# One fused attention and gated-MLP kernel on Trainium2: the first batch's v and u products as plain fp32 matmuls, two more pairs on the sums of v, small work moved to ScalarE, and a new order of all tasks

## The chip, the cores and the metric

The kernel runs on one core of one Trainium2 chip. The metric is the time of one execution on the device, in microseconds (us); what counts is the median of several runs. The trace is that of one profiled execution.

The engines of the core are PE (TensorE, matrix products), DVE (VectorE), ACT (ScalarE), POOL (GpSimd) and SP (SyncE, which here only issues DMAs). Each works through its own instructions in program order; semaphores hold one back until what it reads is there. PEld is the loading of weights into PE, which runs beside the matmuls.

## What is computed

```
# q, k, v: (8 batches, 8 heads, 576 positions, 64)
q_d, k_d, v_d = means over 4 neighbouring positions
out_d   = softmax(scale * q_d @ k_d.T) @ v_d          # 144 positions, then each repeated 4 times
out_loc = softmax(scale * q @ k.T where |i-j| < 4) @ v
x = (repeat(out_d) + out_loc)  as (8, 576, 512)
h = gelu(x @ w_in);  u, v = halves of h                # w_in 512 x 1024
v = layer_norm(v) * g;  v = w_sg @ v + b_sg            # w_sg 576 x 576
out = x + (u * v) @ w_out                              # w_out 512 x 512
```

All is fp32 at full accuracy; the MLP's weights arrive as 64-bit floats.

## The kernel before, in words

**Attention** runs over 32 pairs of heads, numbered g = 0 to 31, four to a batch. For a pair, SP loads q (`lq`), k (`lk`), the pooled v (`lv`) and the windows of v (`lw`). `qs` and `ks` add q and k over four positions. `S`, `Y`, or both as `YS`, are the local and the pooled scores on PE (L629, L650). Then come the softmax (`mx`, `ma`, `mb`, `my`, `ea`, `eb`, `ec`, `re`, `rc`), its normalization (`np` for the local, `nq` for the pooled probabilities, L725 and L728), the transposes `T`, `U`, `t` on PE (L731, L740) with their copies out of PSUM (`pa`, `pb`, `pc`, `pe`), and `D` (`av`, L792 for the pooled part, L808 for the local part). `oe`, `od`, `xa`, `xb` merge both into x. For the first EARLY_D pairs `D` multiplies with the four rows of v that make a mean, one after the other, straight from what was loaded. For all others `vs` adds the four first (L613 and L614 on POOL, L610 on DVE) and `D` needs a quarter of the pooled matmuls. `lv` is issued as four DMAs of 48 rows in the first case, as two of 112 rows in the second.

**The MLP** runs per batch. Each fp32 operand is split into a high part, rounded to fp32r, and a low part, the rest: x by `xh`, `xl` and `xc`, the weights by `wh` and `wl`. A product is then three fp32r matmuls: high by high, high by low, low by high. `v` (L916) makes five tiles of 128 positions (the last has 64) by 512 columns, over four chunks of 128 of the inner dimension. In batch 0 each chunk is a task of its own, `vk<tile>.<chunk>`, and the last is `v0.<tile>`, so that chunk k can start when pair k is done. `u` (L1114) makes eight blocks of 128 by 288, `s` (L1068; in batch 0 by L1114) is the product with w_sg, and `o` (L1243) that with w_out.

**Weights** come as 64-bit words. For each of twelve blocks (`y0` to `y3` for v, `z0` to `z3` for u, `r0` to `r3` for w_out) `wu` and `wq` scale the words' halves, `wb` shifts bits on DVE (L407 and L409), `wt` adds the halves on POOL (L417), which gives the fp32 weight; `wh` and `wl` (L424) split it.

**The order** is a text, `ORDER`: one list of about 2,450 task names, each with the engine it goes to where there is a choice. `place` walks it, hands out the buffers (8 PSUM banks, 10 wide and 38 narrow SBUF buffers) and so fixes each engine's program. Nothing is moved at run time. Every DMA waits until the sixth before it has landed (`DEPTH`), and `lv` waits for the `D` of two pairs before (of one pair before from g = 6 on).

```
fs = range(FAC if early_d else 1)            # L784: 4 or 1 matmuls per pooled block
ops += [(xh, 0, k), (xh, 1, k)] + ([] if last else [(xl, 0, k)])     # L914: three fp32r products
add(N("lv"), dq2, load_v4, [N("D", ahead // 2)], ...)                # L836
```

Of the kernel before, what the change touches and what calls it, by code (L numbers as in the profile page):

```python
# [90 lines left out]
wy0 wuy0 wqy0/V wby0 wty0 wz3 wqz3 wbz3 lk0 lq0 qs0 S0 mx0 lk1 lq1 S1 ks0/P Y0 lq2 ks1/P ia0 ib0 wuz3 wy1 ea0 mx1 wqy1  # L91
my0 ny0 ec0 es0 qs2 lk2 lk3 lq3 wy2 S2 qs1/P mx2 wtz3 ia1 whz3 ib1 Y1 ea1 wz0 re0 why0 wqy2 ks2/P ia2 wlz3 my1 ny1 ec1
wuy1 ib2 rc0 es1 lq4 wuz0 S3 wqz0 lv0 ks3/P qs3/P Y3 np0/V T0 mx3 lw0 nq0 U0 re1/V rc1 np1 lk4 ia3 ib3 nq1 ea3 Y2 qs4/P
wbz0 ea2 T1 pa1 pa0 wtz0 pb0 my2 pc0 small t0 pe0 wby2 wuy2 wty2 ny2 ec2 es2 my3 ny3/V U1 pb1 pc1/V re2 rc2 t1 whz0
ks4/P ec3 pe1 D0 oe0 es3 wby1 re3 od0 nq2 why2 YS4 wy3 wuy3 lq5 np2 wqy3 qs5 lv2 U2 T2 pa2 wty1 xa0 rc3 why1 nq3 t3 xb0
np3 wlz0 my4 ny4 t2 pb2/V wby3 ma4 pc2 lv1 lw1 xh0 xl0/P ec4 U3 wly2 T3 pa3 wty3 mb4 pb3/V wz2 pc3/V lk5 pe2 mx4 pe3 ks5
wqz2 wbz2 wuz2 D1 YS5 ma5 my5 oe1 od1 xa1 xb1 mb5 lw2 mx5 wly0 D2 oe2/V lv4 od2 xh1/V lw3 vk1.0 vk2.0 nx4 eb4 ea4 re4
rc4 lv3 D3 xa2 xl1 wtz2 whz2 wly1 vk1.1 nx5 vs4 ea5 eb5 xb2 xh2 ny5 nq4 wz1 oe3/V od3 xa3 xb3 xh3 xc0 why3 wly3 ec5
vk0.0 vk3.0 vk3.1 xl3/P lk6 vk0.1 lq6 wlz2 np4/V T4 xl2 U4 qs6 wr2 ks6 wqz1 pa4/V re5 rc5 wuz1 vk1.2 wbz1 wtz1 v0.1 wqr2
vg0.1 vk0.2 vk2.1 vk2.2 np5 lw4 pb4 t4 pc4 xc1 pe4 v0.2 wbr2 xc2 vg0.2 wq3 whq3 wq1 D4 vb0.1 vb0.2 xc3 whq1 wlq1 vp0.2  # L100
YS6 ma6 my6 wur2 v0.0 vg0.0 vk4.0 vk4.1 ny6 vk4.2 v0.4 nq5 vk3.2 wq0 whq0/V wlq0 ec6 v0.3 lk8 t5 whz1/V wlz1 mb6 mx6
wlq3 vb0.0 lk7 T5 pa5/V U5 ks7 pb5/V pc5/V va0.4 lq7 vp0.0 oe4/V qs7 vn0.2 lv5 lq8 vs5 od4 xa4 nx6 eb6 ea6 vg0.3 vj0.4
xb4 pe5 ks8 u0.3 vn0.0 u0.4 u0.2 ua0.4 vg0.4 vp0.1 ua0.2 vn0.1/A ua0.3 re6/V lw5 rc6 nq6 u0.5 qs8 wr1 wqr1/V D5 wq2
oe5/V lv6 ua0.5 vh0.0 od5 YS7 my7 ma7 mb7 whq2 t6 xa5 u0.0 vb0.4 np6 U6 vb0.3/A T6 u0.6 vh0.1 xb5 ny7 ec7 wlq2 mx7 wq4
pa6/V pb6 pc6 vs6 whq4 pe6 vl0.1 vh0.2/V vp0.4 lw6 vl0.0 u0.7 vn0.4 u0.1 ua0.6 ua0.7 b vp0.3 vn0.3/A ua0.0 vl0.2 ua0.1
vh0.4/V D6 YS8 wlq4/V nx7 eb7 vh0.3/V vl0.3/P ea7 lv7 lk10 wbr1 wtr2 vl0.4 s0.1 ma8 oe6/V od6 s0.0 xh5 lw7 vs7 s0.5 mb8
my8 ny8 mx8 nx8/V lk9 sa0.1 ec8 re7/V rc7 nq7/V xa6 xb6 np7 wr0 wqr0 wur1 sa0.0 sm0.0/P s0.2 ks10 lq10 lw8 t7 T7 pa7 ks9
U7 s0.3 pb7/V pc7 sm0.1/P pe7/V lq9 sa0.2 eb8 gh0.0/A qs9 sa0.3 sm0.3 ea8 sa0.5 D7 YS9 qs10 wr3 wur3 s0.4 ma9 xl5 re8
rc8 wtr1 s0.6 whr2 mb9 xh4 my9 lv8 oe7 sm0.2/P vs8 lk11 np8 T8 ny9 ec9 sa0.4 nq8/V lw9 xc5 mx9 U8 pa8 pb8 pc8/V t8 pe8
xh6 nx9 wqr3 s0.7 od7 xa7 xb7 eb9 lq11 sm0.5/P D8 lv9 YS10 lk12 sm0.4/P sa0.6 xh7 wur0 xl4/P xc4 xl6/P xc6 sa0.7 sm0.7  # L110
wbr0 xl7 oe8 ea9 my10 ny10/V ks12 wtr0 re9 rc9 ec10 ks11 v1.3 ma10 whr0 gh0.1/A vg1.3 np9/V mb10 mx10 wlr2 sm0.6/P
gh0.3/A br v1.0 nq9 od8 whr1 gl0.1 qs11/P xc7 wbr3 gh0.2/A bd vs9/V v1.1 vg1.1 vb1.1/A gl0.2/V T9 xa8 pa9 t9 wlr1 U9
pb9/V pc9/V pe9 v1.2 xb8 vg1.0 vb1.0/A vg1.2 wlr0/V nx10 vb1.2/A gl0.3/V wtr3 u1.4 lq12 D9 lv10 YS11 gl0.0/V oe9/V vp1.0
gr vn1.0/A vb1.3/A u1.5 ua1.4 whr3 od9 xa9 tq2 my11 qs12/P ma11 mb11 ua1.5 v1.4 ny11 ec11 vs10 tq3 xb9 mx11 vp1.1
vn1.1/A tq4 bs wlr3/V be nx11 eb10 eb11 tq1 o0.2 o0.1 ea10 ea11 u1.6 ua1.6 vp1.3 vn1.3/A vp1.2 o0.6 gt o0.4 o0.0 re10
# [1381 lines left out]
```

## Time and profile before

| | |
|---|---|
| median of 3 runs | 561.27 us (560.44 to 561.32) |
| profiled execution | 562.39 us, span of the trace 560.6 us |
| PE busy | 536.9 us, 96% of the span |
| DVE, ACT, POOL busy | 483.5 (86%), 417.4 (74%), 364.0 (65%) |
| DMA | 64.50 MB, mean 115 GB/s |

The span is the time from the first to the last instruction of the trace; the execution's own time has 1.8 us around it. The profile also cuts the span into 40 slices of 14 us and gives each engine's busy tenths: PE shows 6, 8, 5 and 8 in the first four and 9 in nearly all others. The clock that PE was granted is near full speed in all slices but the third and fourth, where it reads 8 tenths.

### The profile page before, as it was taken

How to read it: one execution, taken by the hardware profiler on the slowest of the kernel's cores; microseconds unless marked ns; L12 is line 12 of the kernel's file. 1: busy time of each engine (PE TensorE's matmuls, PEld its weight loads, DVE VectorE, ACT ScalarE, POOL GpSimd, SP SyncE). 2: the span in 40 equal slices, each digit the busy share in tenths (PEclk: the TensorE clock that was granted, in tenths of full speed). 3: DMA queues.
4: the chain of work that ended last, by engine and by line, in shares of the span. 5: the costliest groups of instructions: out<-in, count | busy, mean ns of one | idle time of the engine just before them, and what ended most of it. 6: DMA issues, size and time to landing. Idle time of an engine off the chain costs nothing.

```text
span 560.6 us, 17562 instructions
## 1 busy us (share of the span) xinstructions
PE 536.9 (96%) x6864; PEld 499.9 (89%) x6864; DVE 483.5 (86%) x1008; ACT 417.4 (74%) x1384; POOL 364.0 (65%) x441
## 2 busy tenths in 40 slices
...
GB/s 314 237 234 318 170 82 278 53 67 105 158 176 122 2 154 110 47 136 42 157 108 77 100 90 122 155 45 57 118 144 135 36 101 109 50 1 2 64 21 107
DMA packets 31923, 64.50 MB, mean 115 GB/s; under 512 B 3808, under 2 KB 4832, under 8 KB 31840
## 3 DMA queue, kind: packets, MB, share of 16 engines
q1 hardware_dynamic: 31840, 63.37, 36.0%
...
q14 instruction: 29, 0.24, 0.1%
...
## 4 chain that ended last, share of the span: by engine, by line
PE 82%; DVE 8%; DMA 6%; issue 3%; ACT 1%; SPq 1%; DVEq 0%; ACTq 0%
PE ps L1114 19%; PE ps L916 17%; PE ps L1068 16%; PE ps L1243 14%; PE ps L792 4%; PE ps L808 3%; PE ps L629 3%; PE ps L731 3%; DMA R<-in_qT_dram 3%; PE ps L650 2%; PE ps L740 2%; DMA R<-in_kT_dram 1%; DMA weight_z<-in_w_in_dram 1%; DMA weight_y<-in_w_in_dram 1%; SPq L240 1%
## 5 line engine op out<-in xcount | busy, mean ns | idle before, releaser
L1114 PE MATMUL ps<-X,weight_z 128*128 128x288 f32 x512 | 109.2, 298 | 1.6 <-DVE X L637 1.6
L916 PE MATMUL ps<-weight_y,X 128*128 128x512 f32 x320 | 97.3, 398 | 0.1
L689 ACT ACTIVATE X<-X,nb 128x64 f32<-128x64 f32 x280 | 93.6, 339 | 1.2 <-DVE nb L668 0.8
L1114 PEld LDWEIGHTS ps<-X,weight_z 128*128 128x128 f32 x512 | 84.1, 188 | 2.2 <-DVE X L637 1.8
L1114 PE MATMUL ps<-R,weight_z 128*128 128x288 f32 x256 | 75.5, 295 | 0.0
L916 PEld LDWEIGHTS ps<-weight_y,X 128*128 128x128 f32 x320 | 58.5, 188 | 12.7 <-ACT R L1142 0.4
L1068 PE MATMUL ps<-wsg_h,R 128*128 128x288 f32 x266 | 58.4, 300 | 0.3 <-ACT pd L711 0.3
L248 ACT CAST R<-R 128x576 fp32r<-128x576 f32 (+2 forms) x77 | 48.0, 646 | 13.7 <-DVE R L1105 5.9
L1250 DVE TENSOR_TENSOR R<-ps,R 128x288 f32<-128x288 f32 x98 | 41.9, 448 | 16.8 <-PE ps L1243 16.6
L689 ACT ACTIVATION_READ_ACCUMULATOR X<-X,nb 128x1 f32 x280 | 53.4, 191 | 0.0
L248 ACT COPY R<-ps 128x464 f32<-128x464 f32 (+4 forms) x94 | 35.0, 412 | 23.2 <-PE ps L731 10.3
L1226 POOL TENSOR_TENSOR R<-R,R 128x576 fp32r<-128x576 f32 x24 | 35.2, 1477 | 26.2 <-ACT R L248 11.7
L916 PE MATMUL ps<-weight_y,R 128*128 128x512 f32 x128 | 50.6, 395 | 0.5 <-DVE R L827 0.5
L1243 PE MATMUL ps<-R,weight_r 128*128 128x288 f32 x336 | 50.3, 297 | 0.0
L1114 PEld LDWEIGHTS ps<-R,weight_z 128*128 128x128 f32 x256 | 48.2, 188 | 0.1
L1243 PEld LDWEIGHTS ps<-R,weight_r 128*128 128x128 f32 x336 | 46.7, 188 | 0.9
L1068 PEld LDWEIGHTS ps<-wsg_h,R 128*128 128x128 f32 x266 | 43.5, 188 | 0.9 <-ACT pd L711 0.6
L1243 PE MATMUL ps<-R,R 128*128 128x288 f32 x252 | 38.6, 299 | 0.8 <-DVE R L470 0.8
L1003 POOL TENSOR_TENSOR R<-R,R 128x512 fp32r<-128x512 f32 (+1 forms) x18 | 24.9, 1393 | 20.9 <-DVE R L248 7.6
L1142 ACT ACTIVATE R<-ps 128x288 f32<-128x288 f32 x64 | 24.5, 412 | 16.8 <-PE ps L1114 15.5
L1243 PEld LDWEIGHTS ps<-R,R 128*128 128x128 f32 x252 | 34.8, 188 | 1.7 <-DVE R L470 1.2
L711 ACT ACTIVATE pd<-ps,nbd 128x144 f32<-128x144 f32 x96 | 35.3, 377 | 0.9 <-DVE nbd L680 0.2
...
## 6 DMA issues: line engine op xcount, KB each, us to landing
...
```

The source lines that it names most:

```text
L248: (nc.scalar.copy if e == "A" else ENG[e].tensor_copy)(**kw)
L689: nc.scalar.activation(out=st["ms"][:, t, :], in_=src, func=AF.Exp, bias=st["nb"][:, t:t + 1], scale=scale, accum_out=sums[par][:, t:t + 1])
L711: nc.scalar.activation(out=pd[:, n], in_=st["sdv"][n].rearrange("p (c k) -> p c k", c=3), func=AF.Exp, bias=st["nbd"][:, n:n + 1], scale=s ...
L792: nc.tensor.matmul(out=out, lhsT=lhsT, rhs=pdt[ks, probs, h * QC:(h + 1) * QC], start=first, stop=last)
L916: nc.tensor.matmul(out=acc, lhsT=r32(l), rhs=r32(weights[f"y{k}"][:, 0, w]), start=(i == 0 and ks[0] == 0), stop=(i == len(ops) - 1 and ks ...
L1003: ENG[e].tensor_tensor(out=r32(dst), in0=vact[s][0][0:n], in1=vh[0:n, 0:DM], op=ALU.subtract)
L1068: nc.tensor.matmul(out=s_bank(j, c), lhsT=r32(l), rhs=r32(r), start=first_in and i == 0, stop=i == len(ops) - 1, skip_group_check=not firs ...
L1114: nc.tensor.matmul(out=acc[:, 0:HALF], lhsT=r32(l), rhs=r32(r), start=(first and n == 0), stop=(last and n == len(ops) - 1))
L1142: nc.scalar.activation(out=gate(i), in_=at["ps", "m", b, "u", i][:, 0:HALF], func=AF.Gelu_apprx_tanh)
L1226: ENG[e].tensor_tensor(out=r32(gl[m]), in0=us[raws[m]], in1=gh[m], op=ALU.subtract)
L1243: nc.tensor.matmul(out=bank(j, c), lhsT=r32(l), rhs=r32(r), start=first and i == 0, stop=i == len(ops) - 1, skip_group_check=not first)
L1250: nc.vector.tensor_tensor(out=x, in0=bank(j, c), in1=x, op=ALU.add)
```

## The change

Five things are changed.

- `EARLY_D` goes from 4 to 2: pairs 2 and 3 add v first (`vs2`, `vs3`), their `lv` are two DMAs of 112 rows, and their `D` have 16 pooled matmul records in place of 64.
- In batch 0 the v and u products are plain fp32 matmuls of x and of the unsplit weight that `wt` leaves: one matmul per chunk in place of three (two in the last v tile). `xh`, `xl` and `xc` are gone for batch 0; chunk k waits for `xb` of pair k and for `wt` of weight k. The splits of the weights stay, for batch 1.
- The last v tile of batch 0 needs no joining of its halves (`va`, `vj` are gone there).
- ACT may do `nq` (as three scaled copies) and `xc`.
- `ORDER` is another list. It starts with loads of q and k where it started with two weights.

```
-EARLY_S, EARLY_D, WIDE, SMALL_O, SMALL_S = 4, 4, 4, 1, 1
+EARLY_S, EARLY_D, WIDE, SMALL_O, SMALL_S = 4, 2, 4, 1, 1
...
+    def unsplit(t):
+        return at["R", "w", t][:, 0:DM]
...
         def norm_d(e):
+            if e == "A":
+                for i in range(3):
+                    nc.scalar.activation(out=st["pdv"][:, i], in_=st["pdv"][:, i], func=AF.Copy,
+                                         scale=st["rc"][:, NT + i:NT + i + 1])
+                return
...
+        if b == 0:
+            return
         add(N("xh"), {"A": 0.64, "V": 0.4}, x_high, ...
...
-        xn = [f"xl{b * NPAIR + p}" for p in range(NPAIR)]
+        xn = [f"{'xb' if first else 'xl'}{b * NPAIR + p}" for p in range(NPAIR)]
...
+                if first:
+                    for k in ks:
+                        l = sb[k]["x"][:, s * P:min(S, (s + 1) * P)]
+                        nc.tensor.matmul(out=acc[0:LEFT] if last else acc, lhsT=l, rhs=unsplit(f"y{k}"), start=k == 0, stop=k == KT - 1)
+                    return
...
+                if first:
+                    acc = buf("ps", "m", b, "u", i)[:, 0:HALF]
+                    for k in range(KT):
+                        l = block(unsplit(f"z{k // 2 * 2 + d}"))[:, k % 2, ds]
+                        nc.tensor.matmul(out=acc, lhsT=l, rhs=sb[k]["x"][:, cs], start=k == 0, stop=k == KT - 1)
+                    return
...
-            w = [f"wly{i}" for i in range(KT)] if first else []
+            w = [f"{'wty' if first else 'wly'}{i}" for i in range(KT)] if b < 2 else []
```

Of the list, the places around pairs 2 and 3 as the engines get them follow. A row names the line, the operation, and what it writes and reads; "x2" is two in a row.

SP before, from pair 2's v (48 rows at a time) to pair 3's v:

```order
L240 DMA R_656<-in_v_dram 48x512 x2
L240 DMA R_657<-in_v_dram 48x512 x2
L240 DMA R_702<-in_v_dram 48x512 x2
L240 DMA R_703<-in_v_dram 48x512 x2
L240 DMA X_708<-in_vw_dram 128x640
L240 DMA weight_z_733<-in_w_in_dram 128x2x512
L240 DMA R_737<-in_kT_dram 128x586
L240 DMA X_845<-in_vw_dram 128x640
L240 DMA R_904<-in_v_dram 112x512
L240 DMA R_905<-in_v_dram 112x512
L240 DMA X_911<-in_vw_dram 128x640
L240 DMA R_934<-in_v_dram 48x512 x2
```

The same stretch of SP in the change:

```order
L240 DMA R_652<-in_v_dram 48x512 x2
L240 DMA X_671<-in_vw_dram 128x640
L240 DMA R_741<-in_qT_dram 128x586
L240 DMA R_750<-in_kT_dram 128x586
L240 DMA weight_y_757<-in_w_in_dram 128x1024
L240 DMA R_760<-in_v_dram 112x512
L240 DMA R_761<-in_v_dram 112x512
L240 DMA R_765<-in_v_dram 112x512
L240 DMA R_766<-in_v_dram 112x512
L240 DMA X_771<-in_vw_dram 128x640
L240 DMA X_833<-in_vw_dram 128x640
```

Pair 5's k (`R_737` before, `R_750` in the change) stood ahead of pair 3's v by six DMAs and still stands ahead of it; pairs 2 and 3 now take four DMAs for v in place of eight, and pair 4's v (`R_904`, `R_905`) has moved behind them.

PE before, where the scores of pair 5 (L629) end and `D2` begins:

```order
L629 MATMUL ps_814<-R_737,R_651 64x64 x2
L629 MATMUL ps_813<-R_737,R_651 64x64 x2
L629 MATMUL ps_814<-R_737,R_651 64x64 x2
L792 MATMUL ps_849<-R_700,R_656 64x144 x2
L792 MATMUL ps_850<-R_700,R_656 64x144 x2
L792 MATMUL ps_849<-R_700,R_656 64x144 x2
```

The same place in the change, where L632 are the scores, L924 the chunks of the plain v product, L748 a transpose and L800 the pooled part of `D2`:

```order
L632 MATMUL ps_791<-R_750,R_741 64x64 x2
L924 MATMUL ps_769<-R_586,R_777 128x512
L748 MATMUL ps_846<-turn_p,pd_102 112x112 x2
L924 MATMUL ps_753<-R_586,R_777 128x512
L924 MATMUL ps_775<-R_586,R_777 128x512
L800 MATMUL ps_863<-R_727,vd_99 64x144 x2
L800 MATMUL ps_864<-R_727,vd_99 64x144 x2
L800 MATMUL ps_863<-R_727,vd_99 64x48 x2
L800 MATMUL ps_864<-R_727,vd_99 64x96 x2
L816 MATMUL ps_863<-R_663,X_771 64x58 x2
```

Three chunks of v now stand between pair 5's scores and `D2` (three more stand ahead of the scores), and `D2` reads the sums `vd_99`.

POOL before, from the normalization of pair 3 (L725) to the sums of v of pair 4 (L613, L614):

```order
L725 TENSOR_TENSOR X_472<-X_472,rc_109 128x640
L424 TENSOR_TENSOR weight_z_542<-R_491,weight_z_542 128x2x256
L827 TENSOR_TENSOR R_712<-R_675,X_710 128x576
L424 TENSOR_TENSOR weight_y_614<-R_516,weight_y_614 128x512
L417 TENSOR_TENSOR R_695<-R_695,weight_y_648 128x512
L424 TENSOR_TENSOR weight_y_361<-R_169,weight_y_361 128x512
L417 TENSOR_TENSOR R_745<-R_745,weight_z_733 128x512
L424 TENSOR_TENSOR weight_y_678<-R_608,weight_y_678 128x512
L613 TENSOR_TENSOR pairs<-R_904 112x256
```

POOL in the change, from the same normalization (L728 there) to the sums of pairs 2 and 3 (L616, L617):

```order
L728 TENSOR_TENSOR X_449<-X_449,rc_109 128x640
L424 TENSOR_TENSOR weight_y_604<-R_582,weight_y_604 128x512
L736 TENSOR_TENSOR pd_102<-pd_102,rc_109 128x9x48
L417 TENSOR_TENSOR R_586<-R_586,weight_y_469 128x512
L424 TENSOR_TENSOR weight_y_638<-R_404,weight_y_638 128x512
L417 TENSOR_TENSOR R_735<-R_735,weight_z_579 128x512
L616 TENSOR_TENSOR pairs<-R_760 112x256
L617 TENSOR_TENSOR vd_99<-pairs 112x128
L616 TENSOR_TENSOR pairs<-R_761 112x256
L617 TENSOR_TENSOR vd_99<-pairs 112x128
L616 TENSOR_TENSOR pairs<-R_765 112x256
L617 TENSOR_TENSOR vd_100<-pairs 112x128
```

The split of x (L827) and two splits of weights have gone from ahead of this place, and the sums of two more pairs have come.

## Rows read from the trace of the kernel before

**Rows 1.** Busy time in stretches: us of each engine (instructions), PE's clock, DMA share, GB/s

```profile
0.00:24.70 24.70, 18.54 (x334) 14.05 (x338) 21.78 (x65) 15.71 (x40) 18.10 (x32) 1.00 0.82 280
24.70:37.47 12.77, 8.73 (x272) 7.51 (x264) 10.93 (x26) 11.32 (x44) 12.69 (x13) 1.00 0.86 253
37.47:45.17 7.70, 5.20 (x127) 5.07 (x128) 3.91 (x9) 3.07 (x17) 5.61 (x7) 0.56 0.80 222
45.17:50.67 5.50, 4.41 (x127) 3.67 (x126) 3.35 (x8) 4.06 (x22) 1.62 (x2) 1.00 1.03 385
52.50:61.39 8.89, 8.89 (x45) 6.95 (x43) 8.30 (x16) 6.73 (x17) 6.19 (x5) 1.00 0.92 265
61.39:112.00 50.61, 50.61 (x841) 48.20 (x841) 45.73 (x104) 47.45 (x170) 42.67 (x53) 1.00 0.46 133
...
140.00:280.00 140.00, 136.87 (x1709) 128.37 (x1709) 130.43 (x267) 115.86 (x381) 95.42 (x114) 1.00 0.35 110
```

**Rows 2.** Timeline of PE, 36 to 53 us: start, duration, what, idle before

```profile
36.76 0.71 PE L650 MATMUL ps<-kd,qd 64*64 64x144 f32 x12 [1.21 <-DVE kd L593]
39.97 0.34 PE L650 MATMUL ps<-kd,qd 64*64 64x48 f32 x1 [2.50 <-issue]
...
46.26 0.56 PE L808 MATMUL ps<-R,X 64*64 64x58 f32 x21 [1.09 <-issue]
...
48.34 1.71 PE L792 MATMUL ps<-R,R 48*64 48x144 f32 x60
...
52.20 0.33 PE L808 MATMUL ps<-R,X 64*64 64x58 f32 x4 [1.52 <-issue]
```

**Rows 3.** Timeline of PE, products of batch 0, a transpose, and D of pair 4

```profile
53.96 0.62 PE L916 MATMUL ps<-weight_y,X 128*128 128x512 f32 x2
...
55.37 0.62 PE L916 MATMUL ps<-weight_y,X 128*128 128x512 f32 x2
...
61.39 0.63 PE L792 MATMUL ps<-R,vd 48*64 48x144 f32 x15
...
68.88 0.43 PE L1114 MATMUL ps<-X,weight_z 128*128 128x288 f32 x2
...
74.45 0.43 PE L1114 MATMUL ps<-X,weight_z 128*128 128x288 f32 x2
...
79.48 0.58 PE L731 MATMUL ps<-turn_l,X 122*128 122x122 f32 x4
```

**Rows 4.** Groups of PE's instructions, 56 to 112 us: busy us, mean ns of one

```profile
L731 PE MATMUL ps<-turn_l,X 122*128 122x122 f32 x25 | 3.6, 267 | 0.0
```

**Rows 5.** Timeline of SP's queue (DMA issues), and the first wait of DVE

```profile
21.70 7.28 SPq L240 DMA_DIRECT2D R<-in_v_dram  x8
...
30.95 1.20 SPq L240 DMA_DIRECT2D R<-in_v_dram  x2
...
34.85 4.10 SPq L240 DMA_DIRECT2D R<-in_v_dram  x4
...
4.83 0.43 DVE L403 TENSOR_SCALAR weight_y<-weight_y 128x512 f32<-128x512 f32 x1 [1.33 <-DMA weight_y<-in_w_in_dram]
```

**Rows 6.** Groups of POOL's instructions, 0 to 52.5 us: busy us, mean ns of one

```profile
L596 POOL TENSOR_TENSOR half<-R 128x288 f32<-128x288 f32 x8 | 5.3, 666 | 0.2
L417 POOL TENSOR_TENSOR R<-R,weight_y 128x512 int32<-128x512 int32 x4 | 5.2, 1297 | 4.6 <-DVE R L409 4.6
L728 POOL TENSOR_TENSOR pd<-pd,rc 128x432 f32<-128x432 f32 x5 | 4.5, 908 | 5.1 <-DVE rc L722 5.1
...
L725 POOL TENSOR_TENSOR X<-X,rc 128x640 f32<-128x640 f32 x3 | 3.8, 1260 | 0.4 <-DVE rc L722 0.4
...
L597 POOL TENSOR_TENSOR kd<-half 128x144 f32<-128x144 f32 x5 | 2.1, 426 | 0.4
...
L613 POOL TENSOR_TENSOR pairs<-R 112x256 f32<-112x256 f32 x2 | 1.5, 738 | 0.0
...
L614 POOL TENSOR_TENSOR vd<-pairs 112x128 f32<-112x128 f32 x2 | 0.9, 456 | 0.2
```

More of the change, by code (lines that the diff above doesn't have):

```diff
@@ L90 @@
 ORDER = """
[L91 to L115, printed above, removed]
@@ new lines @@
+lv0 wz3 ny3 U1 rc2 t1 ec3 re3 pa1 pb1 pc1 pe1 D0 wz0 wby2 wby1 oe0 nq2 np2 T2 wqz0 rc3 od0 xa0 xb0 wty2 why2 YS4 why0 U2
+ma4 t2 np3 lv1 wly2 T3 pa2 mb4 wuy1 my4 pb2 ny4 lw1 D1 pc2/V pe2 wuz0 mx4 pa3 wbz0 ec4 lq5 nq3 U3 pb3 lk5 oe1/V vk2.0
+pc3/V wy3 od1 lv2 wty1 lv3 vk1.0 lw2 wqz3 ks5 vk0.0 xa1 qs5 YS5 wuz3 xb1 wbz3 wly0 wtz0 nx4 vk1.1 my5 vs2 ma5 mb5 lw3
+wqy3 vs3 ea4 t3 pe3/V eb4 re4 vk2.1 ny5 ec5 vk0.1 D2 mx5 wby3 lq6 wtz3 D3 nx5 oe2/V od2 oe3/V vk3.0 lk6 vk3.1 xa2 xb2
+od3 vk3.2 vk0.2 wz1 lk7 wuy3 ea5 whz3/V eb5 vk1.2 whz0 why1/V wty3 why3 wlz3 wqz1 xa3 xb3 v0.1 rc4 vk2.2 re5/V nq4/A rc5
@@ new lines @@
+whq4/V D5 YS7 wlq4 wur2 vb0.4 vp0.4 vl0.2/P wq1 my7 oe5/V U6 ny7/V lw6 pa6 whz1 wlz1 lv6 pb6/V pc6 u0.7 ec7 small u0.0
+ma7 mb7 od5 wq3 whq3 wlq3 xa5 xb5 mx7 vs6/V t6 u0.1 ua0.7 whq1 b pe6/V whz2 lk8 ks8 D6 YS8 vn0.4/A ua0.0 ua0.1 vl0.3/P
+nx7 eb7 lv7 wlq1/V lq10 vh0.4/V xh5/V vl0.4/P xl5/P oe6/V lk10 s0.3 od6 gr wtr1 ma8 mb8 mx8 ea7 re7 nx8/V lq9 eb8 wlz2
+ea8 vs7/V s0.0 rc7 np7 nq7 s0.1 lk9 xa6 xb6 ks10 sa0.0 s0.2 U7 my8 ny8 sa0.1 t7 ec8 qs9 sm0.0/P sa0.2 T7 sm0.1/P sa0.3
+wtr2 pa7 pb7/V pc7/V ks9 sm0.3/P pe7 s0.5 lw7 re8 D7 YS9 wr3 whr1 lk11 lw9 rc8 xh6 np8 sa0.5 lv8 vs8/V ma9 nq8/A mb9 lw8
@@ L874, in attention @@
         add(N("np"), {"P": 1.42, "V": 0.78}, norm, [N("rc")])
-        add(N("nq"), {"P": 0.98, "V": 0.5}, norm_d, [N("rc")])
+        add(N("nq"), {"P": 0.98, "V": 0.5, "A": 1.1}, norm_d, [N("rc")])
         add(N("T"), {"T": 0.44}, turn, [N("np")], takes=[("ps", "t", g, 1)], gives=[("X", "ms", g)])
@@ L927, in emit @@
                 vact[s] = [v]
-                if s == NS - 1:
+                if s == NS - 1 and first:
+                    total = dict(accum_out=sum5[s][0:LEFT]) if by_scalar(s) else {}
+                    nc.scalar.activation(out=v[0:LEFT], in_=acc[0:LEFT], func=AF.Gelu_apprx_tanh, **total)
+                elif s == NS - 1:
                     copy(e, out=v[0:LEFT], in_=acc[LEFT:P])
@@ L1321, in mlp @@
                     add(f"vk{s}.{k}", {"T": c / KT}, v_mm(s, range(k, k + 1)),
-                        xn[k:k + 1] + w[k:k + 1] + (xc[k:k + 1] if last else []) + ([f"vk{s}.{k - 1}"] if k else []),
-                        takes=[] if k else [("ps", "m", b, "v", s)])
+                        xn[k:k + 1] + w[k:k + 1] + ([f"vk{s}.{k - 1}"] if k else []),
+                        takes=[] if k else [("ps", "m", b, "v", s)], gives=[("R", "w", f"y{k}")])
                 add(N("v", s), {"T": c / KT}, v_mm(s, range(k + 1, KT)),
-                    xn[-1:] + w[-1:] + (xc[-1:] if last else []) + [f"vk{s}.{k}"], gives=xs)
+                    xn[-1:] + w[-1:] + [f"vk{s}.{k}"], gives=[("R", "w", f"y{KT - 1}")])
             else:
@@ L1328, in mlp @@
                     gives=xs)
-            if last:
+            if last and not first:
                 add(N("va", s), {"A": 0.58, "V": 0.6}, v_act(s), [N("v", s)], takes=[("R", "v", b, s)])
```

207 lines of the change are left out of this document (112 added, 95 removed).

## The prediction

> **What bounds the kernel now.** Read the stretches first [rows 1]. From 52.5 to 112 us PE is busy without a gap, and from 140 to 280 us for 136.87 of 140 us: PE sets the time there, and only less PE work or fewer of its few waits would help. Before 52.5 it is different. PE is busy for 18.54 of the first 24.7 us and for 8.73 of the next 12.77, while DVE (21.78 and 10.93) and POOL (18.10 and 12.69) are nearly full: there PE waits for the softmaxes and the weights that these two prepare.
>
> Then read PE's timeline around pairs 2 and 3 [rows 2]. It waits 1.21 us for pair 5's pooled k, whose scores stand ahead of `D2` in its program, and then three times, 2.50, 1.09 and 1.52 us, for nothing that the profile shows ("issue"). Between the first two of these there are 127 matmul records [rows 1], between the second and third again 127: PE stops at equal distances in its own program, so I take them for waits for the next block of its code, while the DMA engines are 80% busy and more. From one restart to the next it is 46.26 - 39.97 = 6.3 and 52.20 - 46.26 = 5.9 us: in this traffic a block did not come faster. In the same stretch the granted clock is 0.56 on average [rows 1], so PE ran most of it at 1.2 of its 2.4 GHz, after having been idle for 2.5 us. `D4` starts at 61.39 [rows 3]; from then on I count PE's work only.
>
> **The price of a plain product.** A split v chunk is three fp32r matmuls of 512 columns. Six of them take 55.37 - 53.96 = 1.41 us [rows 3], so one is 0.235, a chunk 0.705 and the last tile (eight matmuls) 1.88. A split u block is twelve of 288 columns: from 68.88 to 74.45 there are 42, 0.1326 each, so 1.59 a block.
>
> No plain fp32 product of full width is in the trace. The nearest are the transposes, plain fp32 and full height: four take 0.58 us [rows 3], of which the last one's own latency is 0.267 [rows 4], so the spacing is 0.313 / 3 = 0.104 us for 122 columns, 0.855 ns a column or two cycles at 2.4 GHz. A plain product leaves two records: `D3` has 60 and then 4 pooled records [rows 2] for 32 products. So a chunk costs 2 x 512 x 0.855 = 0.875 us and a u block 4 x 2 x 288 x 0.855 = 1.97. The bounds: two records at the fp32r pace (0.47 and 1.06) below, four at that pace (0.94 and 2.12) above. I take the transposes because they are the same type at the same height.
>
> The Trainium skill ("FP8 and Floating Point Precision", section TensorE Precision Notes) says that true fp32 takes four passes through the array where the reduced form takes one; that speaks against this change, four against the three of the split. By it a chunk would cost 0.94 and a u block 2.12, and the sum below would end 2.1 us later. The trace agrees in part: two records per product, each at two cycles a column.
>
> So PE's work grows. v: 20 x 0.875 - (16 x 0.705 + 1.88) = +4.3. u: 8 x (1.97 - 1.59) = +3.0. `D2` and `D3` lose 48 records each at 1.71 / 60 = 0.0285 us [rows 2], -2.7. Net +4.6 us. A gain must come from the waits of the first 61 us.
>
> **When D3 can start in the changed order.** Three queues decide.
>
> - POOL. The first q can be there at 5.0 us: the first load, 512 KB, was there at 4.83 [rows 5], and k and q of pair 0 are 586 KB. From then to the sums of pair 3's v the order gives POOL 9 sums of q or k (0.666 + 0.426), 4 x 1.260, 4 x 0.908, 4 weights' `wt` at 1.297, 2 splits of weights, put at the same, and 4 x (0.738 + 0.456) for `vs2` and `vs3` [rows 6]: 9.8 + 5.0 + 3.6 + 7.8 + 4.8 = 31.0. Without a wait that ends at 36.0. I add 1.5 for waits on the first softmax: 37.5.
> - Loads. Up to pair 3's window the change loads twelve q and k (293 KB), six weights (512), 2 x 384 and 2 x 448 of v and four windows (320): 9,532 KB or 9.76 MB, at the 280 GB/s of the first 24.7 us [rows 1] 34.9 us, so landed at 35.6. Pieces of 48 rows hold SP's queue: eight took 7.28 and four 4.10 us, two of 112 rows 1.20 [rows 5]; pairs 2 and 3 save 3.6 + 4.1 - 2 x 1.2 = 5.3 us of that queue. Pair 5's k, the load that PE waited for, comes 1.7 MB sooner (with it, 7,184 KB are loaded in place of 8,892).
> - PE's code. The same count of records puts the next two block ends inside pair 5's scores and inside `D3`. If the first is passed at 33, the second is not before 39 (6.0 on), so `D3`, begun at 37.5, pauses for some 1.4 us.
>
> DVE is close behind POOL; ahead of `D3` it loses one weight's shift, two sums of q, a normalization and a rounding of x and gains a sum of k, so I cost it at no more than POOL's wait. If that cover is gone, `D3` follows DVE instead.
>
> `D3` takes 1.1 as the small `D` do and ends at 37.5 + 1.1 + 1.4 = 40.0. Between it and `D4` PE has ten chunks (8.75) and 14 transposes (1.5): `D4` starts at 50.2, **11.2 us earlier** than 61.39. They have their weights by then: the last one's `wt` is POOL's second task behind `vs3`.
>
> **After D4.** Before, three chunks, the last tile, eight u blocks and a transpose group are left, 2.1 + 1.9 + 12.7 + 0.4 = 17.1; now four chunks and eight u blocks, 3.5 + 15.8 = 19.3: **+2.2**. From 52.5 to 112 us DVE (8.30 + 45.73 of 59.50) and ACT (6.73 + 47.45) are both 91% busy [rows 1], so a PE that runs 9 us ahead will sometimes wait for them: **+2.0**, between -3 (the new order takes work from DVE, where 3.1 us of PE's time is idle from 140 to 280) and +4. `nq` and `xc` on ACT and the last tile without its join I cost at nothing: PE's queue covers them; a single one on the path would be about 1 us, POOL's 0.908 [rows 6] being the nearest.
>
> **Sum.** 560.6 - 11.2 + 2.2 + 2.0 = 553.6 us of span. The median of the runs, 561.27, stood 0.7 above the span (the profiled execution, 562.39, stood 1.8 above), so 554.3 us.
>
> **Rivals.**
>
> 1. *The loads, not the engines, set the pace.* `lv3` may not be issued before `D1` has ended, and both windows stand behind it on SP. If `D1`, which still takes v in 48-row pieces, ends after 38 us, `D3` stays where it was, and PE's added work is all that is left: 561.27 + 4.6 = 565.9, slower. It decides if pair 3's window lands after 47 us, a rate of 211 GB/s; against it, the slowest of the stretches up to 37.47 shows 253 GB/s [rows 1].
> 2. *Part is given back.* PE does little between 12 and 27 us in the new order. If its clock falls as it did from 37.47 on [rows 1], then `D1`, six chunks, pair 5's scores and `D2` (2.2 + 5.25 + 0.9 + 1.1 = 9.5 us at full clock) take up to as much again, of which POOL's queue covers about half. Or ACT and DVE hold PE after `D4` by their upper bound. Either gives some 4.5 more: 558.8, between 556.5 and 562.
> 3. *More is won.* The waits after `D4` end at -3 in place of +2: 549.3.
> 4. *The price is wrong.* At the lower bound ten chunks save 4.1 and the rest 8.9: 541. At the upper one 556.4. Two records at one cycle would contradict the transposes' spacing, so I give the lower end little.
>
> **Chances and range.** Forecast 0.44, rival 2 0.24, rival 3 (with the low price) 0.18, rival 1 (with anything as bad) 0.14. A measurement of this kernel can tell 0.2%, 1.1 us, from no change: 560.2 to 562.4 counts as the same, which takes 0.04 of rival 2. Faster is 0.44 + 0.18 + 0.20 = 0.82, slower 0.14. The range of 547.5 to 562.0 leaves out most of rival 1 and the low price.
>
> **What would show it.** Right: `D3` ended near 40 and `D4` begun near 50; PE without gaps from there; a chunk of L924 every 0.875 us and a block of L1143 every 1.97; one "issue" wait in or near `D3`, not three. Wrong: `D3` after 45 with SP waiting for `D1`; a granted clock near 0.5 between 25 and 40; DVE or ACT as PE's releasers from 50 to 110; chunks at 0.47 or 0.94.

## The result, and the profile after

The changed kernel takes 555.84 us (median of 7 runs, 553.72 to 559.32) where the kernel before, beside it, takes 560.65 (559.36 to 562.61): a ratio of 0.990, with a 95% interval of 0.988 to 0.993. It is 1% faster; 554.3 was forecast, between 547.5 and 562.0. The profiled execution took 556.03 us and its span is 554.2, against 560.6.

The same stretches as in [rows 1], of the kernel after:

```profile
0.00:24.70 24.70, 20.84 (x406) 16.13 (x407) 19.41 (x62) 15.44 (x52) 19.20 (x36) 1.00 0.86 283
24.70:37.47 12.77, 12.07 (x247) 8.53 (x246) 11.62 (x28) 11.37 (x47) 12.15 (x14) 1.00 0.99 274
37.47:45.17 7.70, 7.70 (x125) 4.30 (x125) 7.38 (x18) 7.60 (x33) 6.05 (x7) 1.00 1.04 317
45.17:50.67 5.50, 5.50 (x28) 3.04 (x27) 5.02 (x9) 4.51 (x12) 5.27 (x7) 1.00 1.05 302
...
61.39:112.00 50.61, 49.70 (x688) 42.98 (x687) 48.56 (x100) 46.92 (x156) 41.83 (x43) 1.00 0.57 172
...
140.00:280.00 140.00, 137.68 (x1759) 129.13 (x1760) 122.30 (x244) 118.50 (x403) 95.81 (x117) 0.99 0.34 104
```

From 24.7 to 50.7 us PE is busy for 25.27 of 25.97 us, where it was for some 18, and the granted clock stays at 1.00 through the stretch that had 0.56. But the engines beside PE are now as full as PE: from 37.47 to 45.17 DVE has 7.38 and ACT 7.60 of 7.70 us, and from 61 to 112 DVE has 48.56 of 50.61 where it had 45.73. That will matter.

PE's timeline of the kernel after, the places of [rows 2] and [rows 3] (start, duration, what, idle before):

```profile
27.61 0.47 PE L739 MATMUL ps<-turn_l,X 122*128 122x122 f32 x3 [0.31 <-issue]
...
33.98 0.64 PE L653 MATMUL ps<-kd,qd 64*64 64x144 f32 x13 [0.39 <-DVE qd L596]
...
38.25 0.63 PE L800 MATMUL ps<-R,vd 48*64 48x144 f32 x15
...
40.39 7.13 PE L924 MATMUL ps<-R,R 128*128 128x512 f32 x16
...
50.61 0.63 PE L800 MATMUL ps<-R,vd 48*64 48x144 f32 x15
...
56.04 6.09 PE L1143 MATMUL ps<-R,R 128*128 128x288 f32 x24
...
98.16 0.63 PE L800 MATMUL ps<-R,vd 48*64 48x144 f32 x15
```

`D2` begins at 38.25, `D3` ends with the row before 40.39, `D4` begins at 50.61 (61.39 before), `D8` at 98.16 (106.4 before). Of the three "issue" waits of [rows 2], 5.1 us together, none is left; one of 0.31 has come at 27.3. The eight chunks that begin at 40.39 are followed by a transpose at 47.36, so a chunk is 0.871 us; the three u blocks from 56.04 to 61.96 are 1.973 each.

POOL, then SP's queue, of the kernel after:

```profile
33.17 0.73 POOL L616 TENSOR_TENSOR pairs<-R 112x256 f32<-112x256 f32 x1 [0.39 <-DMA R<-in_v_dram]
...
37.66 0.46 POOL L617 TENSOR_TENSOR vd<-pairs 112x128 f32<-112x128 f32 x1
```

```profile
18.58 1.86 SPq L240 DMA_DIRECT2D R<-in_v_dram  x4
...
26.45 2.50 SPq L240 DMA_DIRECT2D R<-in_v_dram  x4
...
29.39 3.15 SPq L240 DMA_DIRECT2D X<-in_vw_dram  x2
```

The sums of pair 3's v are done at 38.1, and the four DMAs of pairs 2 and 3 hold SP's queue for 2.50 us where eight held it for some 7.7, half of 7.28 and 4.10 [rows 5].

So the lead in the traces is 10.8 us at `D4`, 8.3 at `D8` and 6.4 at the end (between the medians it is 4.8; the profiled execution of the kernel before was one of its slower ones). The rest of this text is on two questions: which part of the change made the 10.8, and what took 4.4 of them away.

### The profile page after: what moved, and what is told of

Same layout as the page of the kernel before. It is cut to its first block, busy times and chain, and to the rows that moved or that the text cites. A ratio compares the mean times of both kernels' runs of the same rounds, so it can differ in the third digit from the quotient of the medians.

```text
span 554.2 us, 17274 instructions
## 1 busy us (share of the span) xinstructions
PE 541.9 (98%) x6720; PEld 492.2 (89%) x6720; DVE 473.6 (85%) x988; ACT 425.7 (77%) x1434; POOL 367.3 (66%) x443
## 4 chain that ended last, share of the span: by engine, by line
PE 82%; DVE 10%; ACT 3%; POOL 3%; issue 1%; ACTq 0%; DVEq 0%; POOLq 0%
PE ps L1086 17%; PE ps L1132 15%; PE ps L1267 14%; PE ps L931 13%; PE ps L800 3%; PE ps L816 3%; PE ps L1143 3%; PE ps L632 3%; PE ps L924 3%; PE ps L739 3%; PE ps L653 2%; PE ps L748 2%; ACT X L692 1%; PE ps L1459 1%; ACT R L248 1%
## 5 line engine op out<-in xcount | busy, mean ns | idle before, releaser
L1132 PE MATMUL ps<-X,weight_z 128*128 128x288 f32 x448 | 96.3, 299 | 0.4 <-ACT R L1166 0.2
L931 PE MATMUL ps<-weight_y,X 128*128 128x512 f32 x280 | 85.0, 397 | 0.5 <-DVE R L409 0.2
L1132 PEld LDWEIGHTS ps<-X,weight_z 128*128 128x128 f32 x448 | 74.3, 190 | 1.4 <-ACT R L1166 0.4
L1132 PE MATMUL ps<-R,weight_z 128*128 128x288 f32 x224 | 66.5, 297 | 0.0
L931 PEld LDWEIGHTS ps<-weight_y,X 128*128 128x128 f32 x280 | 51.0, 188 | 11.3 <-DVE R L1226 0.5
L1021 POOL TENSOR_TENSOR R<-R,R 128x512 fp32r<-128x512 f32 (+1 forms) x26 | 34.2, 1318 | 26.1 <-ACT R L248 7.7
L248 ACT COPY R<-ps 112x192 f32<-112x192 f32 (+4 forms) x86 | 32.4, 411 | 24.4 <-DVE R L248 6.3
L931 PE MATMUL ps<-weight_y,R 128*128 128x512 f32 x112 | 44.1, 394 | 0.0
L613 DVE TENSOR_REDUCE vd<-R 112x128 f32<-112x512 f32 x42 | 43.7, 1082 | 0.3 <-DMA R<-in_v_dram 0.3
L1132 PEld LDWEIGHTS ps<-R,weight_z 128*128 128x128 f32 x224 | 42.6, 190 | 0.0
```

Of the source, the lines that this page charges most:

```text
L248: (nc.scalar.copy if e == "A" else ENG[e].tensor_copy)(**kw)
L613: nc.vector.tensor_reduce(out=vd[:, i], in_=v.rearrange("p f d -> p d f"), axis=AX.X, op=ALU.add)
L931: nc.tensor.matmul(out=acc, lhsT=r32(l), rhs=r32(weights[f"y{k}"][:, 0, w]), start=(i == 0 and ks[0] == 0), stop=(i == len(ops) - 1 and ks ...
L1021: ENG[e].tensor_tensor(out=r32(dst), in0=vact[s][0][0:n], in1=vh[0:n, 0:DM], op=ALU.subtract)
L1132: nc.tensor.matmul(out=acc[:, 0:HALF], lhsT=r32(l), rhs=r32(r), start=(first and n == 0), stop=(last and n == len(ops) - 1))
```

## The experiments

All kernels that were run; D4 and D8 are the starts of these two in the trace, in us. A name that begins with b is an edit of the kernel before, one that begins with a an edit of the changed kernel. Each ran beside the kernel before on the same chip, whose medians were 560.65 to 561.83.

| kernel | median us | ratio to before, 95% interval | span | D4 | D8 |
|---|---|---|---|---|---|
| before | 560.65 | 1 | 560.6 | 61.4 | 106.4 |
| changed | 555.84 | 0.990 (0.988 to 0.993) | 554.2 | 50.6 | 98.2 |
| b_early2 | 560.83 | 0.999 (0.997 to 1.001) | 558.4 | 59.4 | 104.4 |
| b_plain | 568.58 | 1.013 (1.010 to 1.017) | 566.1 | 61.0 | 111.2 |
| b_both | 565.37 | 1.007 (1.004 to 1.009) | 563.6 | 59.7 | 110.0 |
| a_early4 | 564.27 | 1.005 (1.002 to 1.008) | 559.5 | 56.7 | 104.2 |
| b_shift | 563.19 | 1.003 (1.001 to 1.005) | 560.9 | 61.5 | 106.9 |
| a_warm14 | 555.85 | 0.990 (0.986 to 0.994) | 553.6 | 50.6 | 98.1 |
| a_less_u | 557.28 | 0.991 (0.988 to 0.994) | 553.8 | 50.3 | 97.9 |
| a_less_v | 555.89 | 0.989 (0.985 to 0.994) | 553.2 | 49.8 | 97.6 |
| a_less_d | 555.34 | 0.990 (0.988 to 0.992) | 554.8 | 51.0 | 98.5 |
| a_less_ud | 557.97 | 0.993 (0.990 to 0.995) | 557.9 | 52.8 | 100.6 |
| a_np9 | 555.07 | 0.990 (0.988 to 0.991) | 553.1 | 50.8 | 98.4 |
| a_nq_pool | 556.94 | 0.992 (0.990 to 0.994) | 555.4 | 50.6 | 98.7 |

### One part alone, in the old order

**b_early2**, the sums of v for pairs 2 and 3 (on DVE, where the change has them on POOL):

```
-EARLY_S, EARLY_D, ... = 4, 4, ...
+EARLY_S, EARLY_D, ... = 4, 2, ...
-... ks5 wqz2 ... lv3 D3 ...
+... ks5 vs2/V wqz2 ... lv3 vs3/V D3 ...
```

> The kernel before with only EARLY_D = 2 (vs2 and vs3 on DVE, one behind ks5, one behind lv3; order otherwise as before). My theory: this part alone takes 2.7 us of records from PE in D2 and D3 and 96 records out of the stretch with the three issue waits, so that one of them (1.1 to 2.5 us) falls out of it; DVE is idle there and takes the 4 sums. D4 begins 3 to 4 us earlier than 61.39, the time is 557 (556 to 559). Rival A, the end is set by the order of the loads alone: within 1 us of the kernel before. Rival B, small DMA pieces were most of the loss: D4 begins 8 us or more earlier, time below 554.

No change that can be measured. PE's timeline of b_early2, at `D3` and `D4`:

```profile
46.26 0.76 PE L794 MATMUL ps<-R,vd 48*64 48x144 f32 x8 [3.15 <-DVE vd L612]
...
59.35 0.63 PE L794 MATMUL ps<-R,vd 48*64 48x144 f32 x15
```

There is no "issue" wait in this stretch any more, and 96 records fewer. But `D3` now waits 3.15 us for the sums of pair 3, whose `lv3` the old list issues just ahead of `D3`. The granted clock was also at 0.50 from 33 to 37.5 us and again behind that wait, from 46.2 to 50. Rival A was nearest: in the old order the part wins 2.0 us at `D4`, and in the medians 0.8, which is none.

**b_plain**, the plain products (in the list only the tasks that are gone are taken out):

```
-        xn = [f"xl{b * NPAIR + p}" for p in range(NPAIR)]
+        xn = [f"{'xb' if first else 'xl'}{b * NPAIR + p}" for p in range(NPAIR)]
-... xh0 xl0/P ec4 ...   (and xh, xl, xc of pairs 0 to 3, va0.4, vj0.4)
+... ec4 ...
```

> The kernel before with only the plain products of batch 0 (xh, xl, xc of pairs 0 to 3 and the join of the last tile taken out of the list, order otherwise as before). My theory: a plain product costs PE more than three fp32r ones, +4.3 us for v and +3.0 for u, and in the old order D3 waits for other things than the splits, so the time goes up by 5 to 7 us: 566 to 568, with D3 ended at 52 as before. Rival C, the gain of the change comes from DVE and POOL having no x to split: D3 or D4 begins at least 4 us earlier and the time is 559 or less.

It is 7.4 us slower (5.6 to 9.3), just above what was expected, and rival C falls. PE's timeline of b_plain:

```profile
39.50 0.25 PE L654 MATMUL ps<-kd,qd 64*64 64x48 f32 x1 [1.94 <-issue]
...
43.60 0.56 PE L817 MATMUL ps<-R,X 64*64 64x58 f32 x21 [1.25 <-issue]
...
50.09 0.32 PE L817 MATMUL ps<-R,X 64*64 64x58 f32 x2 [1.64 <-issue]
...
61.01 0.64 PE L801 MATMUL ps<-R,vd 48*64 48x144 f32 x15
```

The three issue waits are back, `D4` is where it was, and from `D4` to `D8` it takes 50.2 us in place of 45.05. The added work gives just that: three chunks at 0.871 for 0.705, four of the last tile at 0.871 for 1.88 together, eight u blocks at 1.973 for 1.59, which is 0.5 + 1.6 + 3.1 = 5.2. In the old order the plain products are paid for in full.

**b_both**, the two edits together:

> The kernel before with both parts, EARLY_D = 2 and the plain products, but in the old order. My theory: the two add up, -3.5 and +6, so 562 to 565, and what the whole change has won beyond that (6 to 9 us) is the new order. Rival D, the parts need no new order: 557 or less.

565.37, just above the range, and slower than the kernel before: the parts do half a percent better together than added up (-0.1% and +1.3%, measured +0.7%). Between b_both and the change lies the new list alone (and with it the small work on ACT): 1.007 to 0.990, 9.3 us. The list is what wins. It does not win without the sums of v, though, as the next run shows; the list with the split products was not run.

### One part undone, in the new order

**a_early4**: `EARLY_D` back at 4, `vs2` and `vs3` out of the list.

> The changed kernel with EARLY_D back at 4 (vs2 and vs3 gone, v of pairs 2 and 3 again in 48-row pieces). My theory: PE is busy without a gap from 27.6 us on, so its 96 extra records cost 2.7 us in full, and SP's queue is some 5 us longer ahead of the windows, which moves D3 from 39.2 to 40 to 43: D4 at 53 to 55.5 in place of 50.6, time 558.5 to 561. Rival E, POOL's sums of v set D2 and D3: without them D2 begins 2 us or more earlier and the time is 556 or less.

It is slower by more than expected: 1.005 against 0.990, 8.2 us, more than the whole gain; its runs spread from 561.3 to 569.2. The trace is of the fastest, and there the 6.1 us at `D4` can be read off. PE's timeline of a_early4, and one stretch of it:

```profile
38.15 1.71 PE L802 MATMUL ps<-R,R 48*64 48x144 f32 x60
...
44.59 0.58 PE L818 MATMUL ps<-R,X 64*64 64x58 f32 x10 [1.89 <-issue]
45.09 8.50 PE L926 MATMUL ps<-R,R 128*128 128x512 f32 x16
...
56.68 0.64 PE L802 MATMUL ps<-R,vd 48*64 48x144 f32 x15
```

```profile
45.09:53.43 8.34, 8.34 (x17) 3.63 (x17) 8.25 (x17) 2.87 (x5) 6.27 (x7) 0.83 1.05 331
```

`D2` begins where it did (38.15), so POOL's sums had not held it: rival E falls. Then come 2.7 us of records, an issue wait of 1.89 inside `D3`, and the eight chunks behind it at a clock of 0.83, 8.34 us in place of 6.97: 2.7 + 1.9 + 1.4 = 6.0. In this execution the price of 96 records is not their 2.7 us alone: the wait, which the next section puts at the end of a block of PE's program, and the clock after it cost more.

### Are the issue waits at fixed places of PE's program?

**b_shift**: the kernel before with 20 of its matmuls on zeros left out.

```
-WARM = {"S0": 28, "S3": 20}
+WARM = {"S0": 28, "S3": 0}
```

> The kernel before with 20 matmul records fewer ahead of S3 (WARM S3 from 20 to 0; they compute nothing that is used). In the kernel before PE restarted from its three issue waits with 596, 723 and 850 records behind it. My theory, they are waits for the next block of PE's program, at fixed counts of records: what issue waits there are come again at 596, 723 and 850, so at other instructions than before, 20 records further down the program (the first behind the pooled scores of pair 5, among its local scores). Time 559 to 562, as D3 is not set by PE's work of the first 20 us. Rival F, the waits belong to what these instructions need: they come at the same instructions, with 576, 703 and 830 records behind them.

PE's records up to the moment of a restart, first column of counts, of the kernel before:

```profile
0.00:39.96 39.96, 27.27 (x596) 21.56 (x596) 33.17 (x90) 29.50 (x97) 33.28 (x46) 0.98 0.84 267
0.00:46.25 46.25, 32.47 (x723) 26.62 (x724) 36.65 (x98) 31.10 (x104) 36.40 (x50) 0.93 0.83 265
0.00:52.19 52.19, 36.89 (x850) 30.30 (x850) 40.27 (x106) 34.52 (x121) 38.02 (x52) 0.93 0.85 277
```

The restart of b_shift, and the records up to it:

```profile
40.77 1.01 PE L629 MATMUL ps<-R,R 64*64 64x64 f32 x25 [2.61 <-issue]
```

```profile
0.00:40.76 40.76, 29.82 (x595) 24.10 (x595) 33.26 (x90) 28.86 (x93) 32.66 (x45) 0.87 0.82 263
```

595, not 576: the wait has moved down the program by the 20 records, from the pooled scores of pair 5 into its local scores. Rival F falls. The waits at 723 and 850 did not come again; one of 1.09 us came at 15.85, with 219 records ahead. The places agree in all programs that showed such a wait (a trace can lack a few records): 219 in b_shift; 471 in the changed kernel, a_less_v and a_less_d; 595 to 598 in the kernel before, b_shift, b_plain, b_both, a_np9 and a_less_ud; 723 or 724 in the kernel before, b_plain, a_less_v and a_less_ud; 850 in the kernel before, b_plain and a_early4. They lie 125 to 127 records apart, or (219 and 471) twice that. The time was somewhat above the 562 that was expected (0.3% slower; the mean clock of its runs is 0.982 to 0.994).

The places are fixed, but whether PE stops there is not. In the changed kernel's trace PE passes 596, 723 and 850 at 34.2, 39.6 and about 51.5 us and stops at none of them. The plain chunks, two records in 0.87 us, stretch the program between the first two, but that this is the reason is not shown: a_less_ud has the same PE program up to there and stops at both, for 0.69 and 1.30 us, while a_less_u and a_nq_pool, which have it too, show no such wait.

The Trainium skill says ("Runtime: NRT & Kernel Launch", Instruction fetch mechanics) that an engine's program is fetched in blocks of 256 instructions and that crossing from one to the next is mostly hidden. The spacing agrees: 127 records, each a weight load and a matmul, are 254 instructions. That it is hidden does not hold for all of them here: where PE stopped in the first 52 us, it stopped for 0.3 to 2.6 us, while the DMA engines were at 79% and more.

### Does PE set the time of the changed kernel?

Its trace says so: PE has no gap of note from 28 to 98 us. Three kernels take work out of PE; the first two leave products out, so they compute another output.

**a_less_u**:

```
-                    for k in range(KT):
+                    for k in (0, KT - 1):
                         l = block(unsplit(f"z{k // 2 * 2 + d}"))[:, k % 2, ds]
```

> The changed kernel with two of the four products left out of each of batch 0's eight u blocks (the chunks of pairs 1 and 2 do not enter u; output not the reference's). It takes 8 x 0.985 = 7.9 us from PE between 56 and 75 us and nothing from another engine. My theory, PE alone sets the time from 28 us on: time 6.5 to 8 us less, 548 to 549.5. Rival H, DVE and ACT (both above 90% busy from 50 to 112 us) take over at once: 4 us less or below, 552 and more, with PE waits of 4 us and more between 60 and 140.

**a_less_v**:

```
                     for k in ks:
+                        if not last and k in (1, 2):
+                            continue
```

> The changed kernel with the chunks of pairs 1 and 2 left out of batch 0's first four v tiles (eight chunks of 0.87 = 7.0 us of PE's work, three ahead of D2 and five between D3 and D4; output not the reference's). My theory: D3 is held by POOL's vs3 (done at 38.1) and begins near 38.2 in place of 39.2, D4 at 45 to 46 in place of 50.6, and the time is 4.5 to 5.5 us less, 550.5 to 551.5. Rival I, the softmax of pair 4 or the loads hold D4 (DMA is at full share from 31 to 50 us): D4 at 48 or later, time 553.5 or more.

**a_warm14**: `WARM` of S0 from 28 to 14.

> The changed kernel with 14 in place of 28 warm-up matmuls ahead of S0. PE runs them until 6.6 us, and S0 begins at 7.10, though POOL could sum q of pair 0 at 4.52. My theory: S0 begins at 5.0 to 5.5, and the chain behind it (DVE's maxima, POOL's normalizations, T2 at 24.49) is up to 1.5 us earlier, so the time is 0.5 to 1.5 us less, 554.3 to 555.3. Rival G, loads or POOL's sums set the pace of the first 25 us, and PE is without its warm-up at half clock: no change or up to 1 us more.

None of the three gains anything: 0.991, 0.989 and 0.990 against the change's 0.990. My theory, that PE alone sets the time, falls with all three, and these are the runs that teach most. PE's timeline of a_less_u, with its waits, and its stretch from `D4` on:

```profile
50.28 0.63 PE L800 MATMUL ps<-R,vd 48*64 48x144 f32 x15
...
62.16 1.21 PE L1143 MATMUL ps<-R,R 128*128 128x288 f32 x4 [1.10 <-DVE R L248]
65.60 0.64 PE L739 MATMUL ps<-turn_l,X 122*128 122x122 f32 x4 [2.22 <-POOL X L728]
73.47 0.41 PE L748 MATMUL ps<-turn_p,pd 112*112 112x112 f32 x2 [0.91 <-ACT pd L714]
...
97.92 0.63 PE L800 MATMUL ps<-R,vd 48*64 48x144 f32 x15
```

```profile
61.39:80.00 18.61, 13.96 (x263) 11.00 (x263) 17.43 (x39) 16.51 (x35) 14.74 (x15) 0.91 0.65 189
```

Of the 7.9 us that were taken out, 4.65 are idle in this stretch (13.96 busy of 18.61, where the change has 18.61). PE waits for a normalization on POOL, an exponential on ACT, a copy on DVE. From `D4` to `D8` it takes 47.6 us, as in the changed kernel. One stretch shows where the rest of the time went. It runs from the transpose that waits for POOL (L739) to the later one at 70.1 us (L748), behind which ACT's next work follows. First PE of the changed kernel, then PE of a_less_u, then the busy times and the clock (0.65) of a_less_u:

```profile
67.25 0.58 PE L739 MATMUL ps<-turn_l,X 122*128 122x122 f32 x4
...
70.08 0.45 PE L748 MATMUL ps<-turn_p,pd 112*112 112x112 f32 x3
```

```profile
65.60 0.64 PE L739 MATMUL ps<-turn_l,X 122*128 122x122 f32 x4 [2.22 <-POOL X L728]
...
70.06 0.45 PE L748 MATMUL ps<-turn_p,pd 112*112 112x112 f32 x3
```

```profile
65.60:70.53 4.93, 4.93 (x121) 4.64 (x122) 4.48 (x12) 3.29 (x7) 4.08 (x5) 0.65 0.53 164
```

POOL let PE go on 1.65 us earlier than in the change. But behind the idle time the clock was granted at 0.65 on average, and the same instructions ended where they end in the change, so nothing was left. In the changed kernel PE has no wait here: its own work fills the stretch to the end, and POOL's chain is 1.65 us shorter. What would come back with less of PE's work and the clock held at 1.00 was not tried.

PE's timeline of a_less_v, at `D4`, and DVE's ahead of it:

```profile
49.84 0.56 PE L800 MATMUL ps<-R,vd 48*64 48x144 f32 x14 [1.01 <-DVE R L248]
```

```profile
47.11 2.03 DVE L613 TENSOR_REDUCE vd<-R 112x128 f32<-112x512 f32 x2
49.06 0.90 DVE L248 COPY R<-ps 128x116 f32<-128x116 f32 x3
```

Seven us of PE's work less, and `D4` comes 0.8 us earlier: DVE works without a pause from 40.8 us, through pair 4's sums of v, to the copies that `D4` reads (an issue wait of 0.84 us inside `D3`, ended at 40.0, had held it). Rivals H and I were right. In a_warm14 `S0` began at 4.95 in place of 7.10 and `D1` 1.4 us earlier, and the lead ended at the sums of v. POOL of a_warm14:

```profile
34.27 0.74 POOL L616 TENSOR_TENSOR pairs<-R 112x256 f32<-112x256 f32 x1 [1.82 <-DMA R<-in_v_dram]
```

POOL waits for pair 2's v to land, `D3` ends at 40.37 as in the change (40.39), and `D4` begins at 50.59.

**a_less_d** takes DVE's work instead (its output, and that of the next kernel, are others too):

```
+                if e == "V" and g < 8:
+                    nc.vector.tensor_copy(out=vd[:, i], in_=v[:, 0])
+                    continue
                 if e == "V":
                     nc.vector.tensor_reduce(out=vd[:, i], ...)
```

> The changed kernel with DVE's sums of v for pairs 4 to 7 replaced by a copy of one row (the pooled outputs of these pairs are not the reference's): eight reductions of 1.07 us become copies of some 0.2 us, about 7 us less of DVE's work between 47 and 100 us, PE's work unchanged. Two kernels that took 7.0 and 7.9 us of PE's work out gained nothing, so my theory is now that DVE (104.1 of the 109 us from 31 to 140) is as full as PE there, two rails of one length: less DVE work alone gains little, as PE's 107.0 of 109 us stay: 554 to 556. Rival J, DVE alone is the bound and PE only fills in: 4 us or more less, 552 or below.

**a_less_ud** is a_less_d with the edit of a_less_u.

> Both at once: two of four products left out of batch 0's u blocks (7.9 us of PE) and DVE's sums of v of pairs 4 to 7 as copies (7 us of DVE); output not the reference's. My theory of two rails: neither alone gains, both together gain 3 to 6 us, 550 to 553, D8 at 92 to 95 in place of 98.2, ended by ACT (98.4 of the 109 us). Rival K, a third rail, ACT's or the loads', is as long as these two: 554.5 or more, D8 not before 97.

a_less_d is where two rails of one length would put it (555.34). Eight copies took 4.4 us where the eight reductions took 8.2, so 3.8 us of DVE's work went, not 7. a_less_ud does not gain either, and of the two rivals K is nearer: from `D4` to `D8` it takes 47.9 us, with 7.9 us of PE's and 3.8 of DVE's work gone. (Its `D4` is 2.2 us late, behind its two issue waits of 0.69 and 1.30 us, so that stretch, not its time, is to be compared.) PE waits 2.22 us for POOL there too, and the granted clock falls behind it (0.72 from 68 to 74 us).

In all nine kernels with the new list this stretch takes 47.5 to 48.2 us, also in a_early4, where it begins 6 us later and the other engines had that much longer to work ahead. So in the changed kernel two things are of nearly one length there: PE's own work, and a chain through POOL and ACT, with what the clock loses when PE waits for it. Neither POOL nor ACT was relieved.

### Two pieces of small work

**a_np9** puts one normalization from DVE on POOL (`np9/V` becomes `np9`).

> The changed kernel with pair 9's normalization on POOL in place of DVE. On DVE it took 3.71 us in the trace where others take 1.07, with DVE full and PE waiting 0.7 us for it; on POOL one takes 1.26. My theory: D9 and what follows come 0.7 to 2.6 us earlier, time 553.5 to 555.2. Rival L, PE and POOL are held by the next of DVE's tasks anyway: no change that can be measured.

**a_nq_pool** puts `nq` of 15 pairs and `xc` of ten, as the list has them on ACT, back on POOL (`nq4/A` becomes `nq4`, and so on).

> The changed kernel with the 15 normalizations of pooled probabilities and the few last columns of x that ACT took over back on POOL. My theory: POOL has room (66% busy), each is covered by PE's queue or costs 1 us at most where it is not (nq4 and nq8, where everything is full): no change or up to 2 us more, 555.5 to 558. Rival M, this part carries the gain: 559 or more.

Neither can be told from the change (0.990 and 0.992 against 0.990, the intervals overlap). In the trace of a_np9 `D11` and all later `D` are 1.1 to 1.7 us earlier than in the change, and the span is 1.1 shorter; the medians, 555.07 and 555.84, do not prove it. Nor is it the edit's doing: `D10` begins at the same time in both (146.39 and 146.40), and what differs behind it is the clock. PE's two waits of the change, then the same stretch of the change and of a_np9:

```profile
146.39 0.47 PE L800 MATMUL ps<-R,vd 48*64 48x144 f32 x8 [0.92 <-ACT R L248]
148.03 0.39 PE L800 MATMUL ps<-R,vd 48*64 48x48 f32 x7 [1.17 <-ACT R L248]
```

```profile
148.00:154.00 6.00, 5.97 (x123) 5.86 (x124) 2.95 (x6) 4.81 (x12) 2.90 (x4) 0.72 0.46 135
```

```profile
148.00:154.00 6.00, 5.96 (x134) 5.84 (x135) 4.33 (x9) 5.94 (x13) 2.90 (x4) 1.00 0.45 135
```

a_np9 has the same two waits (0.90 and 1.17), and its clock stays up. a_nq_pool lies within what was expected, so the small work on ACT does not carry the gain.

## Why the prediction was right, and where it was right for the wrong reason

- **What bounded the kernel.** Right for the first 50 us. The waits there were PE's loss, and they are what went: PE's idle time ahead of `D4` falls from 15.3 to 4.6 us.
- **The price of a plain product.** Right: 0.875 and 1.97 were put, 0.871 and 1.973 measured, and b_plain paid it. Four passes, as the Trainium skill has it ("FP8 and Floating Point Precision", TensorE Precision Notes), were priced at the fp32r products' pace, 0.94 and 2.12. The number of passes is not contradicted: 0.871 us for 512 columns are 4.1 cycles a column at 2.4 GHz, where an fp32r product took 1.1.
- **POOL's rail**, 37.5: the sums ended at 38.1. But undoing them (a_early4) did not move `D2`, which PE's own chunks held, and a_warm14 shows v's landing right behind. Around 38 us three rails end within about a microsecond of each other.
- **The loads**, landed at 35.6: `D3` waited for none of them. The 5.3 us of SP's queue that pairs 2 and 3 would save were some 5.2.
- **PE's code.** The mechanism, waits at fixed counts of records, was right and is now shown. The pause of 1.4 us inside `D3` did not come: `D3` met the block's end at 39.6, 5.4 us behind the last one, and passed it. In a_less_ud it did come (1.30), so its absence is in part luck. My bound of 6 us a block was too high: b_plain went from one restart to the next in 4.1.
- **`D4` at 50.2**, 11.2 us earlier: 50.61 and 10.8.
- **After `D4`, +2.2 of PE's work and +2.0 of waits.** The sum, 4.2, is right (4.4 measured), but one of its terms is so by luck. From `D4` to `D8` PE is busy without a gap in both kernels, 45.05 us before and 47.55 after: +2.5, PE's work, near what was counted. That I counted "PE's work only" was wrong all the same: with 7.9 us of that work gone nothing came back, since POOL's chain is only 1.65 us shorter and the clock took those. The waits for DVE and ACT are the step that failed. None came up to `D8`, and behind `D8` PE is idle for no more than before (7.8 us, 8.4 before). What was lost there, 1.9 us, is nearly all clock: behind PE's waits for ACT at 146 and 148 us it was 0.72 over 6 us, and a_np9, where it did not fall, goes from `D10` to `D11` in 12.9 us in place of 14.5.
- **The rivals.** Rival 1 did not come: v of pairs 2 and 3 left SP's queue from 26.45 to 28.95, before `D1` had ended at 30.4, so the wait on which it rested is not there. That `lv` waits for the `D` of two pairs before is a rule of the list's order, and no wait at run time: the kernel before issued pair 4's v at 30.95 [rows 5], and its `D2` began at 41.3. Rival 2's first half, the clock, did not come up to 112 us (1.00), and came at 148 instead; its second half, other engines holding PE behind `D4`, came only when PE was given less work. Rival 3 would have needed the waits behind `D4` to pay, and that part cost 4.4. Rival 4, another price, falls with the 0.871.

What would the split products cost in the new order? They would take 2.5 us of work from PE there and put the splits of x back on engines that are as full. That was not run, since the list would have to be planned anew for it.
